# Layer 2's input weights decoded from layer 1's second tile pair on, and layer 1's third pair summed in one group

## The chip, the core and the metric

One core of a Trainium2 chip runs the whole program. The metric is the device time of one execution in microseconds (us); runs are compared by their median. TensorE (PE) multiplies, VectorE (DVE) and ScalarE (ACT) do the elementwise work, GpSimd (POOL) copies a little at the start, and nearly all transfers are issued by SyncE (SP) on one queue.

## The reference, cut to what matters

Three stages follow each other. Chunked attention (4 batches, 8 heads, 768 positions, chunks of 32 with a small context) gives x of 3072 tokens by 512. Two feed-forward layers of the same form follow, each with its own weights:

```
x = attention(q, k, v, mem_k, mem_v)            # 3072 x 512
h = x @ moe_w_in;   g = h * clip(h + 3, 0, 6) / 6;                x = g @ moe_w_out
h = x @ moe2_w_in;  g = where(h >= 1, h, where(h <= -1, 0, (h + 1)**2 / 4));  out = g @ moe2_w_out
```

w_in is 512 x 2048 and w_out 2048 x 512. The weights reach the kernel as float64 words, and TensorE is given pairs of fp32r tiles, a high part and the rest (hi, lo), so that each product is three matmuls: hi by hi, hi by lo, lo by hi.

## The kernel before, in words

**Tiles.** The tokens are 6 tiles of 512. Tiles 0 and 1 of layer 1 go through it plainly while attention for the later tiles runs between them. From tile 2 on, two tiles are taken as a pair, and each product with w_in is made with 7 instead of 8 block products (`PRODUCTS`: A11, S1, S2, A12, S3, S4, A22, where the S are sums of blocks). The pairs are named (layer, pair): (0, 1), (0, 2), (1, 0), (1, 1), (1, 2), with layer 1 as 0 and layer 2 as 1. "Layer 1's second tile pair" is (0, 1), its third (0, 2), and the first of layer 2 is (1, 0).

**f pairs.** The 2048 hidden columns are 16 blocks f of 128, taken two at a time: 8 f pairs, 0 to 7. `hidden_pair` makes one f pair: 7 products of 6 matmuls (L1027 to L1029) into PSUM banks `ph`, three copies by ACT (L1010), three additions by DVE (L1014), and four gates (`gate`: ACT L1074, in layer 2 also L1078, and DVE L1082). The banks of one product are taken again by a later one, so TensorE waits where a copy or an addition has not yet read a bank.

**The way out.** Pair (0, 1) multiplies each gated tile with w_out plainly (`project`, L902 to L904, after a split into hi and lo by ACT L886 and DVE L887). The other four pairs are in the table `SEVEN`: they keep their gated tiles g (up to 16 of them, in the pool of 32 slots `w` that also holds weights, raw words and operands) and sum w_out with 7 products too (`out_pair`, matmuls L1264 to L1266, block sums L1224, splits L886 and L887). `SEVEN` says in which groups of f pairs that is done. Within a group each product runs over the group's f pairs into two PSUM banks `po`, and then both banks are read out into the sums `csum`: the first time by a copy (L1234 on ACT or L1236 on DVE), later by an addition on DVE (L1242). Before the change (0, 2) has two groups of four f pairs: four f pairs, their way out, four f pairs, their way out.

**Decoding.** Layer 2's weights are decoded while layer 1 runs. `weight_pair(i)` takes f pair i of w_in: two loads of raw words (L318), a shift (L325 on ACT or L327 on DVE), a rescaling (ACT L331), a join (DVE L335), four differences (DVE L457), the casts (ACT L468, L471, L472) and the rests (DVE L469, L473, L476), and four stores to `wfs` (L482). `weight(1, f, 1)` does the like for w_out (casts on ACT at L303, rests on DVE at L366, stores L380), and `combine_out(i)` makes the block differences of w_out (DVE L496 and L510, ACT L509, stores L515). Nothing of this is multiplied before (1, 0) begins.

**What sets the order.** `Plan` is a list scheduler that runs when the program is built: every task has an engine or a choice of two, an estimated length, buffers, the tasks it depends on, and a key. Among what can start, the smaller key goes first. The result is one fixed order of instructions on each engine, and one queue of transfers on SP; at run time each engine takes its instructions in that order and waits where an input is late. A key counts in units of one plain f block; `base` is the key at which a pair begins, `NK` that of (0, 1), and `done[n, i]` is the last product of f pair i of the n-th pair.

Of the kernel before, what the change touches and what calls it, by code (L numbers as in the profile page):

```python
# [38 lines left out]
NK = 2 * NF  # L39
# [210 lines left out]
def dve(n, fast=False):  # L250
    return 70 + n / (1.92 if fast else 0.96)
# [10 lines left out]
def fused_kernel(ctx: ExitStack, tc: tile.TileContext, qkv, qk, vv, wpk, const, out):  # L262
# [31 lines left out]
    def tile_of(b):  # L294
        if b.tile is None:
            pool = ps if b.slot.pool in banks else smalls if b.slot.pool == "sm" else sb
            b.tile = pool.tile(b.shape, b.dtype, tag=f"{b.slot.pool}{b.slot.n}", name=b.name)
        return b.tile
# [3 lines left out]
    def cast(eng, out, in_):  # L302
        A.copy(out, in_) if eng == "ACT" else V.tensor_copy(out, in_)  # L303
# [6 lines left out]
    def words(raw):  # L310
        t = tile_of(raw)
        u = t.bitcast(U32).rearrange("p (n t) -> p n t", t=2)
        v = t.bitcast(F32).rearrange("p (n t) -> p t n", t=2)
        return u[:, :, 0], u[:, :, 1], v
# [34 lines left out]
    def weight(l, f, z, key, after=()):  # L349
        if l:  # L350
            raw = Buf(["w"], [128, 512], I64, "raw", ("raw", 4), w=1)
            w = Buf(["w"], [128, 2, 512], F32R, "w", ("wq", 4))
        else:
            raw = Buf(["w"] + ["lv"] * (f >= NF - 2), [128, 512], I64, "raw", w=6 if f < 6 else 1)
            w = Buf(["w"], [128, 2, 512], F32R, "w")
        w_buf[l, f, z] = w
        lo, hi = decoded(l, f, z, key, after, raw)

        to = (lambda h: by_chunk(tile_of(w)[:, h])) if l else (lambda h: tile_of(w)[:, h])
        of = (lambda: in_rows(words(raw)[2][:, 1])) if l else (lambda: words(raw)[2][:, 1])  # L360

        def high(e):
            cast(e, to(0), of())

        def low(e):
            V.tensor_tensor(out=to(1), in0=of(), in1=to(0), op=ALU.subtract)  # L366

        add(("ACT", 560), key - 0.2, high, [hi], [(w, 0)])
        t = add(("DVE", dve(512)), key - 0.1, low, [hi, (w, 0)], [(w, 1)])
        if l == 0:  # L370
            last_w.append(t)
        if l:
            keep(l, f, z, key + 1)
        return raw

    def keep(l, f, z, key, after=()):
        w = w_buf[l, f, z]
        to, of = (wos[l, f], ("wos", l, f)) if z else (wis[f], ("wis", f))
        add(
            ("SP", 430), key, lambda e: nc.sync.dma_start(to, tile_of(w).bitcast(F32)),  # L380
            [(w, 0), (w, 1)], [of], kb=512, after=after,
        )
# [681 lines left out]
    def gate(l, p, t, f, key, h, psum=False):  # L1064
# [22 lines left out]

    raw_g = {}
    SEVEN = {
        (0, 2): ((0, 1, 2, 3), (4, 5, 6, 7)), (1, 0): (tuple(range(8)),), (1, 1): (tuple(range(8)),), (1, 2): (tuple(range(6)), (6, 7)),  # L1090
    }
    BASE = (0, 29.25, 57.25, 85.25, 113.25)
    GMOST = 20
# [223 lines left out]
    for s in range(NS):  # L1317
        n, i = divmod(s, m)
# [36 lines left out]
    step = 2.75  # L1355
# [6 lines left out]
    done, w_of = {}, {}  # L1362
    pairs = [(0, 1), (0, 2), (1, 0), (1, 1), (1, 2)]
    for n, (l, p) in enumerate(pairs):
        base = NK + BASE[n]
# [37 lines left out]
            pair_x(*pairs[n + 1], base + 25, [done[n, 7 if seven else 5]], ["w"] if seven else ["in", "lv", "w"])  # L1403
        if n == 0:
            for i in range(NF // 2):
                weight_pair(i, base + 22 + 4 * i, [done[0, 5]])
        if n == 1:
            for i in range(NF // 2):
                raws = [weight(1, 2 * i + x, 1, base + 20 + step * (i + 0.5 * x) - 3, [done[1, 3]]) for x in range(2)]
                combine_out(i, raws, base + 20 + step * (i + 0.5) + 1)  # L1410

    with tc.manual_schedule():
# [98 lines left out]
```

## Time and profile before

| | |
|---|---|
| median of 3 runs | 1062.2 us (1061.84 to 1065.2) |
| the profiled execution's own time | 1067.35 us |
| its span, first to last instruction | 1065.3 us |
| granted TensorE clock, mean | 0.998 of full speed |

The profiled execution is a single one, taken with the profiler on. Its span is 2.05 us shorter than its own time, and its own time is 5.15 us above the median; times within the profile are counted from the span's start.

### The profile page before, as it was taken

The numbers are of one execution on the slowest core, as the hardware profiler recorded it, in microseconds if no ns is written. First come the engines' busy times: TensorE is split into PE (matmuls) and PEld (weight loads), VectorE is DVE, ScalarE is ACT, GpSimd is POOL, SyncE is SP. The second block draws the span as 40 slices with busy tenths as digits, with TensorE's granted clock in tenths as the row PEclk, the third lists the DMA queues.
The fourth block names the chain that finished last, engine by engine and source line by source line (L and its number), as shares of the span: only waits on it lengthen the run. The fifth ranks groups of instructions, "written<-read, shape, count | busy, mean of one in ns | idle before, by whom it ended". The sixth has DMA issues, their size and how long they took to land.

```text
span 1065.3 us, 19872 instructions
## 1 busy us (share of the span) xinstructions
PE 1036.6 (97%) x7381; PEld 842.6 (79%) x7381; DVE 835.9 (78%) x1439; ACT 679.8 (64%) x1427; POOL 27.2 (3%) x49
## 2 busy tenths in 40 slices
PE   6899999999999999999999999999999999999998
PEld 5677787788878887878778788888888888888886
DVE  4897489856876689789899997799765899658654
ACT  5897457634655586666785698655577655676461
POOL 4220000000000000000000000000000000000000
PEclk9999999999999999999999999999999999999999
DMA  8999878873988689999899799855774755965603
GB/s 244 345 358 359 332 237 273 285 243 112 321 282 258 198 300 368 417 399 390 309 404 399 282 344 391 311 178 188 228 266 151 282 169 177 334 223 198 191 34 79
DMA packets 153760, 289.18 MB, mean 271 GB/s; under 512 B 12352, under 2 KB 97984, under 8 KB 153664
## 3 DMA queue, kind: packets, MB, share of 16 engines
q1 hardware_dynamic: 153232, 287.62, 76.9%
q8 instruction: 58, 0.95, 0.4%
q10 hardware_dynamic: 432, 0.30, 0.1%
q14 instruction: 38, 0.31, 0.1%
HBM read 206.08 MB, written 81.79 MB: 270 GB/s over the span
## 4 chain that ended last, share of the span: by engine, by line
PE 67%; DVE 16%; DMA 11%; ACT 3%; issue 2%; SPq 1%; POOL 0%; DVEq 0%; POOLq 0%; ACTq 0%
PE ph L1027 10%; PE ph L1028 9%; PE ph L1029 9%; PE po L1265 7%; PE po L1266 7%; PE po L1264 7%; DMA raw<-wpk 5%; DVE glo L887 4%; PE py L902 3%; PE py L904 3%; PE py L903 3%; DVE raw L335 2%; PE ph L866 2%; DVE g L1224 2%; PE ph L868 2%
## 5 line engine op out<-in xcount | busy, mean ns | idle before, releaser
L886 ACT CAST ghi<-g 128x512 fp32r<-128x512 f32 x234 | 145.0, 621 | 119.1 <-PE po L1266 78.8
L887 DVE TENSOR_TENSOR glo<-g,ghi 128x512 fp32r<-128x512 f32 x234 | 158.7, 686 | 37.5 <-ACT ghi L886 37.2
L1027 PE MATMUL ph<-xop,wf 128*128 128x512 f32 x448 | 175.2, 391 | 3.2 <-DVE s L1014 1.9
L1028 PE MATMUL ph<-xop,wf 128*128 128x512 f32 x448 | 174.5, 390 | 0.8 <-DVE xop L977 0.8
L1029 PE MATMUL ph<-xop,wf 128*128 128x512 f32 x448 | 174.4, 389 | 0.0
L1265 PE MATMUL po<-glo,ws 128*128 128x512 f32 x420 | 163.6, 390 | 0.4 <-DVE glo L887 0.4
L1266 PE MATMUL po<-ghi,ws 128*128 128x512 f32 x420 | 163.4, 389 | 0.0
L1264 PE MATMUL po<-ghi,ws 128*128 128x512 f32 x420 | 163.4, 389 | 0.0
L1074 ACT ACTIVATE r<-s,bias 128x512 f32<-128x512 f32 x120 | 86.6, 724 | 58.7 <-DVE s L1014 57.8
L1014 DVE TENSOR_TENSOR s<-s,ph 128x512 f32<-128x512 f32 x120 | 81.8, 685 | 43.4 <-PE ph L1029 36.5
L1027 PEld LDWEIGHTS ph<-xop,wf 128*128 128x128 f32 x448 | 84.1, 188 | 24.1 <-DVE s L1014 4.2
L902 PE MATMUL py<-ghi,w 128*128 128x512 f32 x256 | 102.5, 401 | 0.0
L1010 ACT COPY s<-ph 128x512 f32<-128x512 f32 x120 | 70.6, 588 | 47.7 <-PE ph L1029 43.8
L903 PE MATMUL py<-glo,w 128*128 128x512 f32 x256 | 100.2, 391 | 0.2 <-DVE glo L887 0.2
L904 PE MATMUL py<-ghi,w 128*128 128x512 f32 x256 | 99.9, 390 | 0.0
L1028 PEld LDWEIGHTS ph<-xop,wf 128*128 128x128 f32 x448 | 84.1, 188 | 18.0 <-DVE xop L977 1.2
L1029 PEld LDWEIGHTS ph<-xop,wf 128*128 128x128 f32 x448 | 84.1, 188 | 17.6
L1265 PEld LDWEIGHTS po<-glo,ws 128*128 128x128 f32 x420 | 78.8, 188 | 17.6 <-DVE glo L887 1.2
L1264 PEld LDWEIGHTS po<-ghi,ws 128*128 128x128 f32 x420 | 78.8, 188 | 16.5
L1266 PEld LDWEIGHTS po<-ghi,ws 128*128 128x128 f32 x420 | 78.9, 188 | 16.1
L1082 DVE SCALAR_TENSOR_TENSOR g<-r,s 128x512 f32<-128x512 f32 x104 | 71.5, 690 | 24.3 <-ACT r L1078 10.1
L1224 DVE TENSOR_TENSOR g<-g 128x512 f32<-128x512 f32 x120 | 81.1, 687 | 1.4
(132 smaller groups left out, 1775.1 us busy)
## 6 DMA issues: line engine op xcount, KB each, us to landing
raw<-wpk SPq DMA_DIRECT2D x64, 512.0 KB
ws<-wcs SPq DMA_DIRECT2D x60, 512.0 KB
wf<-wfs SPq DMA_DIRECT2D x48, 512.0 KB
ws<-wos SPq DMA_DIRECT2D x90, 256.0 KB
wf<-wfs SPq DMA_DIRECT2D x48, 384.0 KB
wos<-w SPq DMA_DIRECT2D x32, 512.0 KB
wcs<-wc SPq DMA_DIRECT2D x32, 512.0 KB
w<-wos SPq DMA_DIRECT2D x32, 512.0 KB
```

Source lines behind the costliest of these rows:

```text
L886: add(("ACT", act(T)), key, lambda e: A.copy(tile_of(ghi), g()), [of], [(ghi, 0)], line="split")
L887: add(("DVE", dve(T)), key + 0.1, lambda e: V.tensor_tensor(out=tile_of(glo), in0=g(), in1=tile_of(ghi), op=ALU.subtract,), [of, (ghi, 0)] ...
L902: P.matmul(y, w2hi, gh, start=first, stop=False)
L903: P.matmul(y, w2hi, gl, start=False, stop=False)
L904: P.matmul(y, w2lo, gh, start=False, stop=last)
L1027: P.matmul(q, whi()[:, m], xh, start=first, stop=False, skip_group_check=True)
L1028: P.matmul(q, whi()[:, m], xl, start=False, stop=False, skip_group_check=True)
L1029: P.matmul(q, wlo()[:, m], xh, start=False, stop=c == 1, skip_group_check=True)
L1224: ("DVE", dve(T)), key, lambda e: V.tensor_tensor(out=o(), in0=i0(), in1=i1(), op=op),
L1264: P.matmul(q, wt[:, 0, m], xh, start=begin, stop=False, skip_group_check=True)
L1265: P.matmul(q, wt[:, 0, m], xl, start=False, stop=False, skip_group_check=True)
L1266: P.matmul(q, wt[:, 1, m], xh, start=False, stop=end, skip_group_check=True)
```

## The change

Three places change. `SEVEN` gives (0, 2) one group of all eight f pairs, so that its eight f pairs come first and its way out after them, as in (1, 0) and (1, 1). `weight_pair` gets smaller keys, wider apart, and may begin when f pair 0 of (0, 1) is done instead of f pair 5. The raw words of layer 2's w_out get smaller keys and may begin after f pair 1 of (0, 2) instead of f pair 3; `combine_out` keeps its keys.

```
     SEVEN = {
-        (0, 2): ((0, 1, 2, 3), (4, 5, 6, 7)), (1, 0): (tuple(range(8)),), ...
+        (0, 2): (tuple(range(8)),), (1, 0): (tuple(range(8)),), ...
...
         if n == 0:
             for i in range(NF // 2):
-                weight_pair(i, base + 22 + 4 * i, [done[0, 5]])
+                weight_pair(i, NK + 6 + 6 * i, [done[0, 0]])
         if n == 1:
             for i in range(NF // 2):
-                raws = [weight(1, 2 * i + x, 1, base + 20 + step * (i + 0.5 * x) - 3, [done[1, 3]]) for x in range(2)]
+                raws = [weight(1, 2 * i + x, 1, base + 14 + 3.2 * (i + 0.5 * x) - 3, [done[1, 1]]) for x in range(2)]
                 combine_out(i, raws, base + 20 + step * (i + 0.5) + 1)
```

TensorE has the same number of instructions before and after, in another order. Three places of the new order follow; rows that begin with - stand only in the order before, rows with + only in the new one.

The first is DVE in (0, 1), at its f pairs 1 and 2. L438 belongs to the weights of (0, 2), L420 to the next of these, L782 and `tr` to attention, and `raw` and `wp` are layer 2's w_in:

```order
+L335 SCALAR_TENSOR_TENSOR raw<-raw 128x512
+L887 TENSOR_TENSOR glo<-s,ghi 128x512
+L1014 TENSOR_TENSOR s<-s,ph 128x512
+L335 SCALAR_TENSOR_TENSOR raw<-raw 128x512
+L457 TENSOR_TENSOR raw<-raw 128x256 x2
+L1082 SCALAR_TENSOR_TENSOR g<-r,s 128x512
+L457 TENSOR_TENSOR raw<-raw 128x256 x2
+L335 SCALAR_TENSOR_TENSOR raw<-raw 128x512
+L303 COPY tr<-tp 128x512
+L1082 SCALAR_TENSOR_TENSOR g<-r,ph 128x512
+L469 TENSOR_TENSOR wp_3788<-raw,wp_3757 128x1024
 L1014 TENSOR_TENSOR s<-s,ph 128x512
```

Between two additions that TensorE's banks wait for there were no rows of layer 2 before; now there are joins, differences and a rest of 1024 columns.

The second is DVE on the way out of (0, 2). Before, in its second group:

```order
L1224 TENSOR_TENSOR g<-g 128x512
L1242 SCALAR_TENSOR_TENSOR csum<-po,csum 128x512
L887 TENSOR_TENSOR glo<-g,ghi 128x512
L1242 SCALAR_TENSOR_TENSOR csum<-po,csum 128x512
L1224 TENSOR_TENSOR g<-g 128x512
L887 TENSOR_TENSOR glo<-g,ghi 128x512
L1224 TENSOR_TENSOR g<-g 128x512
```

After, in the one group:

```order
L887 TENSOR_TENSOR glo<-g,ghi 128x512
L366 TENSOR_TENSOR w<-raw,w 128x512
L335 SCALAR_TENSOR_TENSOR raw<-raw 128x512
L887 TENSOR_TENSOR glo<-g,ghi 128x512
L1224 TENSOR_TENSOR g<-g 128x512
L887 TENSOR_TENSOR glo<-g,ghi 128x512
L1236 TENSOR_SCALAR csum<-po 128x512
L887 TENSOR_TENSOR glo<-g,ghi 128x512
```

The read-outs of `po` come half as often (28 before, 14 after, of which DVE has 23 and 10), and some of w_out's decoding now stands between the splits.

The third is SP's queue in (0, 1), around the first loads L410 of `w` from `wis` (for (0, 2)'s weights). `wos` holds layer 1's w_out, `wf` operands of (0, 2), `q_sb` attention's queries. Before:

```order
L410 DMA w<-wis 128x1024 x2
L566 DMA wf_3780<-wts 128x1024
L566 DMA wf_3786<-wts 128x1024
L566 DMA wf_3788<-wis 128x1024
L566 DMA wf_3796<-wis 128x2x256
L574 DMA w<-wos 128x1024
L632 DMA q_sb<-qk 128x4x128
```

After:

```order
L410 DMA w<-wis 128x1024 x2
L482 DMA wfs<-wp_3757 128x1024
L482 DMA wfs<-wp_3788 128x1024
L482 DMA wfs<-wp_3778 128x768
L574 DMA w<-wos 128x1024
L632 DMA q_sb<-qk 128x4x128
L637 DMA q_sb<-qk 128x384
```

The stores of layer 2's w_in (and, elsewhere in the queue, its raw words) now stand between the transfers of attention and of layer 1's weights; one early load of (0, 2)'s operands goes later.

## Rows read from the trace of the kernel before

**Rows 1.** The page, part 1: the span, and each engine's busy time.

```profile
span 1065.3 us, 19872 instructions
PE 1036.6 (97%) x7381; PEld 842.6 (79%) x7381; DVE 835.9 (78%) x1439; ACT 679.8 (64%) x1427; POOL 27.2 (3%) x49
```

**Rows 2.** Windows by stage: stretch, length, busy us (instructions) by engine, clock, DMA share, GB/s.

```profile
core 0: us, PE busy (x) PEld busy (x) DVE busy (x) ACT busy (x) POOL busy (x), PEclk, DMA share, GB/s
271.10:324.10 53.00, 53.00 (x599) 42.22 (x601) 39.80 (x79) 31.35 (x93) 0.00 (x0) 1.00 0.89 301
324.10:377.50 53.40, 53.40 (x595) 43.27 (x594) 33.56 (x63) 30.53 (x90) 0.00 (x0) 1.00 0.73 227
377.50:434.70 57.20, 56.96 (x367) 45.97 (x366) 53.46 (x87) 43.35 (x74) 0.00 (x0) 1.00 0.94 351
434.70:476.00 41.30, 40.17 (x175) 32.41 (x174) 33.34 (x58) 28.13 (x47) 0.00 (x0) 1.00 1.03 407
476.00:523.60 47.60, 47.60 (x211) 39.43 (x210) 44.63 (x77) 32.34 (x55) 0.00 (x0) 1.00 0.93 342
523.60:554.80 31.20, 29.27 (x127) 23.30 (x126) 27.86 (x49) 25.29 (x44) 0.00 (x0) 1.00 1.05 403
554.80:605.40 50.60, 49.56 (x217) 40.30 (x216) 50.50 (x74) 28.74 (x44) 0.00 (x0) 1.00 0.92 353
605.40:652.50 47.10, 46.77 (x204) 38.17 (x205) 44.05 (x82) 44.25 (x76) 0.00 (x0) 1.00 0.95 353
671.50:757.30 85.80, 85.80 (x380) 70.89 (x380) 77.40 (x123) 48.05 (x75) 0.00 (x0) 1.00 0.62 214
```

**Rows 3.** TensorE's waits from 390 to 650 us: waiter, releaser, us in total, times, longest.

```profile
PE ph L1027 <- DVE s L1014: 1.9, 4, 0.7
PE ph L1027 <- ACT s L1010: 1.3, 1, 1.3
PE ph L1028 <- DVE xop L977: 0.8, 1, 0.8
PE po L1265 <- DVE glo L887: 0.4, 1, 0.4
```

**Rows 4.** Timeline of PE in f pair 2 of (0, 2): start, us, instruction, idle before.

```profile
468.02 0.39 PE L1029 MATMUL ph<-xop,wf 128*128 128x512 f32 x1
468.82 0.50 PE L1027 MATMUL ph<-xop,wf 128*128 128x512 f32 x1 [0.41 <-DVE s L1014]
```

**Rows 5.** Timeline of DVE at the same place.

```profile
466.33 1.22 DVE L469 TENSOR_TENSOR wp<-raw,wp 128x1024 fp32r<-128x1024 f32 x1
467.47 0.69 DVE L1082 SCALAR_TENSOR_TENSOR g<-r,s 128x512 f32<-128x512 f32 x1
468.08 1.28 DVE L1014 TENSOR_TENSOR s<-s,ph 128x512 f32<-128x512 f32 x2
```

**Rows 6.** Timeline of ACT before the longest of these waits, f pair 5 of (0, 2).

```profile
527.01 0.67 ACT L325 ACTIVATE raw<-raw 128x512 uint32<-128x512 uint8 x1 [1.98 <-DMA raw<-wpk]
530.99 0.58 ACT L1010 COPY s<-ph 128x512 f32<-128x512 f32 x1
```

**Rows 7.** Groups of DVE, 271.1 to 324.1 us: busy, mean ns, idle before, its releasers.

```profile
L438 DVE TENSOR_TENSOR wt<-q,wt 128x1024 fp32r<-128x1024 f32 x4 | 4.8, 1208 | 0.3 <-ACT wt L437 0.3
L1082 DVE SCALAR_TENSOR_TENSOR g<-r,s 128x512 f32<-128x512 f32 x3 | 2.1, 693 | 3.6 <-ACT r L1074 3.6
L303 DVE COPY tr<-tp 128x512 f32<-128x512 f32 x3 | 2.1, 689 | 2.3 <-PE tp L789 2.3
```

**Rows 8.** Groups of DVE over the whole span, same columns: the operations that move.

```profile
L335 DVE SCALAR_TENSOR_TENSOR raw<-raw 128x512 uint32<-128x512 uint32 x64 | 44.4, 705 | 2.7 <-ACT raw L331 2.5
L1242 DVE SCALAR_TENSOR_TENSOR csum<-po,csum 128x512 f32<-128x512 f32 x20 | 13.3, 684 | 0.0
L457 DVE TENSOR_TENSOR raw<-raw 128x256 f32<-128x256 f32 x32 | 12.4, 422 | 0.5
L469 DVE TENSOR_TENSOR wp<-raw,wp 128x1024 fp32r<-128x1024 f32 x8 | 9.8, 1220 | 0.0
L473 DVE TENSOR_TENSOR wp<-raw,wp 128x512 fp32r<-128x512 f32 x8 | 5.5, 685 | 0.0
L476 DVE TENSOR_TENSOR wp<-raw,wp 128x256 fp32r<-128x256 f32 x8 | 3.3, 418 | 0.0
```

More of the change, by code (lines that the diff above doesn't have):

```diff
@@ L1089, in fused_kernel @@
     SEVEN = {
-        (0, 2): ((0, 1, 2, 3), (4, 5, 6, 7)), (1, 0): (tuple(range(8)),), (1, 1): (tuple(range(8)),), (1, 2): (tuple(range(6)), (6, 7)),
+        (0, 2): (tuple(range(8)),), (1, 0): (tuple(range(8)),), (1, 1): (tuple(range(8)),), (1, 2): (tuple(range(6)), (6, 7)),
     }
@@ L1405, in fused_kernel @@
             for i in range(NF // 2):
-                weight_pair(i, base + 22 + 4 * i, [done[0, 5]])
+                weight_pair(i, NK + 6 + 6 * i, [done[0, 0]])
         if n == 1:
             for i in range(NF // 2):
-                raws = [weight(1, 2 * i + x, 1, base + 20 + step * (i + 0.5 * x) - 3, [done[1, 3]]) for x in range(2)]
+                raws = [weight(1, 2 * i + x, 1, base + 14 + 3.2 * (i + 0.5 * x) - 3, [done[1, 1]]) for x in range(2)]
                 combine_out(i, raws, base + 20 + step * (i + 0.5) + 1)
```

## The prediction, made before the change was run

> **What bounds the kernel now.** I read the page first: TensorE is busy for 1036.6 us of a span of 1065.3 [rows 1], so a change that leaves its work alone can only shorten the gaps between its matmuls. Where they are, the windows by stage show; I set their bounds at DVE's additions L1014, so that a stage holds whole f pairs. Undisturbed, 380 matmuls take 85.80 us (way out of (1, 0)), 0.2258 us each [rows 2]. A stage without attention loses its length less its matmuls at that price: f pairs 0 to 2 of (0, 2), 41.3 - 175 x 0.2258 = 1.8 us; its first way out, 0.0; f pairs 4 to 6, 2.5; second way out, 1.6; f pairs 0 to 4 of (1, 0), 1.0 [rows 2]. That is 6.9 us in 218, and nearly all that such a change can win. The two stages of (0, 1) ahead of it show no idle TensorE at all (53.00 of 53.00, 53.40 of 53.40) [rows 2].
>
> The waits say who is late: DVE's additions, ACT's copies, DVE's operands for (1, 0), DVE's splits [rows 3]. Two places show how. In f pair 2 of (0, 2) a matmul starts 0.80 us after the one before it, 0.41 of it idle, waiting for an addition [rows 4]; that addition was ready earlier, but stood behind a rest of layer 2's w_in (L469, 1.22 us) and a gate [rows 5]. In f pair 5 ACT waited 1.98 us for late raw words, everything behind that slipped, and the copy L1010 came at 530.99 [rows 6]; this is the wait of 1.3 us in [rows 3]. So decoding that stands in front of an addition or a copy is what costs, and it costs where DVE is nearly full: 50.50 us busy of 50.60 in the second way out, 27.86 of 31.20 before it [rows 2]. DVE has room in (0, 1): 39.80 of 53.00 and 33.56 of 53.40 [rows 2].
>
> **What an instruction of DVE costs.** Two additions in a row take 1.28 us together [rows 5], while one alone is 0.685; the second starts 0.60 after the first, so in a full queue a row costs about 0.9 of its length. I use that factor on sums of rows that I count in the new order.
>
> [...]
>
> **The change, part by part.**
>
> *One group for (0, 2).* Seven products are read out once instead of twice: 28 read-outs become 14, on DVE 23 become 10. 13 x 0.684 [rows 8] x 0.9 = 8.0 us of DVE go. On the new way out, from the first addition of f pair 7 to the first of (1, 0), I count 90.4 us of rows, 81.4 in time, against 378 matmuls, 85.3 us: 95% full, with 11.8 us of rows of w_out's decoding in it. The way out of (1, 0) ran at 77.40 of 85.80 without loss, the old second group at 50.50 of 50.60 with 1.6 lost [rows 2]. I take 0.7, between 0 and 1.6. The matmuls are the same; a longer group costs TensorE nothing by itself. It holds 16 tiles g instead of 8, in 32 slots; (1, 0) does that already, without loss on its way out.
>
> *w_in earlier.* Each f pair of w_in is 2 joins, 4 differences and three rests on DVE: 2 x 0.705 + 4 x 0.422 + 1.220 + 0.685 + 0.418 [rows 8] = 5.4 us of rows. In the new order three f pairs stand in the stretch 271.1 to 324.1 (f pairs 1 to 3 of (0, 1)), where none was: 16.3 us of rows come, 2.1 leave (one L438 and two copies `tr` [rows 7] move out, small ones move in), net 14.2 x 0.9 = 12.8. DVE would have 39.8 + 12.8 = 52.6 us of work in 53.0. In the next stretch 5.1 of rows come, 33.56 + 4.6 = 38.2 of 53.4. The stretch of f pairs 0 to 2 of (0, 2) loses 12.0 of rows and is left with 33.34 - 10.8 = 22.5 us for 39.5 of matmuls, so its 1.8 us should go entirely.
>
> What hides the 12.8 us is DVE's idle time in (0, 1); if DVE lags there, the next thing late is an addition, so a bank, so TensorE. I counted it addition by addition: rows of DVE between two additions x 0.9, against TensorE's work between the products that they read. In the old order DVE's surplus never exceeds 2.0 us in (0, 1), and TensorE shows no idle there [rows 2]. In the new one it has 41.3 us against 37.3 from the first addition of f pair 1 to the second of f pair 3, and with 0.6 carried in reaches 4.5. What exceeds the 2.0 that cost nothing is my price: 2.5 us. The bounds are 0 and 12.8.
>
> The transfers: a pair of w_in is two loads of 512 KB and stores of 2 x 512 and 2 x 384 KB, 2.9 MB. Three pairs more in the 106 us of the two stretches are 81 GB/s on top of 301 and 227, so some 380 and 310; the stage from 434.7 sustained 407 [rows 2]. DMA is close to full but not over; I price nothing, and leave late raw words to the range.
>
> *w_out earlier.* Its decoding fills f pairs 2 to 6 of (0, 2), which now follow each other without a way out between them. f pairs 3 to 6 have 40.7 us of rows, 36.6 in time, for 168 matmuls, 37.9 us: 97% full. The nearest row is 523.6 to 554.8, the same mix, 27.86 of 31.20 with 2.5 lost in three f pairs [rows 2], 1.3 of it by the late raw words [rows 3, 6]. I take 1.5; bounds 0.5 and 3.3 (2.5 x 4/3). Less is left for (1, 0): its first five f pairs have 44.2 us of rows instead of 50.1, and I halve its 1.0 to 0.5.
>
> **The sum.** Before 1.8 + 0.0 + 2.5 + 1.6 + 1.0 = 6.9 us. After: 2.5 in (0, 1), 0 + 1.5 in (0, 2), 0.7 on its way out, 0.5 in (1, 0): 5.2. The difference is -1.7 us. The profiled execution took 1067.35 us in its own time (span 1065.3 [rows 1] and 2.05 around it), and would take 1065.6; it lies 5.15 above the median of the runs, and on that median, 1062.2, the forecast is 1060.5 us. The three runs of before lie 0.3% apart, so 0.3% (3.2 us) is about what this measurement can tell from no change; 1.7 is inside it.
>
> **Rivals.**
>
> *The backlog in (0, 1) is absorbed.* Between its products TensorE has plain projections and attention to do, and half of DVE's idle time there is waiting: 3.6 us of gates for ACT, 2.3 us of `tr` for TensorE [rows 7]; a DVE that runs late finds these inputs ready. Then (0, 1) loses 0, f pairs 3 to 6 lose 0.5, and after is 1.7: -5.2 us, 1057.0. For it: surpluses of up to 2.0 cost nothing before. Against: 99% full for 53 us, and a surplus of 1 to 1.6 us was enough for stalls in (0, 2).
>
> *DVE cannot use its idle time in (0, 1): slower.* Place: 271 to 324. The 13.2 us in which DVE is idle there are waits for inputs in a chain DVE, ACT, DVE, and ACT gets shifts, rescalings and casts of the same three f pairs on top of 31.35 us [rows 2]. If the waits stay, the decoding adds to the stretch instead of filling it. At 70% of 12.8, 9.0 us are lost: -6.9 + 2.7 + 9.0 = +4.8, 1067.0. It decides (slower by more than 3.2) from a loss there of 7.4, 58% of the added work. For it: that fullness, and late raw words that stop a whole engine [rows 6]. Against: the way out at 50.50 of 50.60 lost only 1.6 [rows 2].
>
> *Each operation of DVE costs its full row: slower.* Then f pairs 1 to 3 of (0, 1) have 57.3 us in 53.0, f pairs 3 to 6 of (0, 2) 40.7 in 37.9, the way out 90.4 in 85.3: 4.3 + 2.8 + 5.1 + 0.5 - 6.9 = +5.8, 1068.0. The two additions in 1.28 us [rows 5] speak against it. [...]
>
> **How the numbers follow.** Forecast 0.42, absorbed 0.36, idle time of no use 0.20, full rows 0.02. The likeliest case's own range is 1059.0 to 1063.0. The range of 1056.5 to 1067.0 reaches to the middle of both neighbours, which leaves out some 0.2: what is faster than the absorbed case, and the upper half of the slower ones. Faster by over 0.3% is 0.36, within it 0.42, slower 0.22.
>
> **What would show it.** In the profile after: TensorE idle at f pairs 1 to 4 of (0, 1), some 2.5 us in all, released by L1014, L1010 or an input of them; DVE over 95% busy there; no idle at f pairs 0 to 2 of (0, 2); few waits on the one way out, and 14 read-outs. The prediction is wrong on the fast side if (0, 1) still shows none, on the slow side if it shows over 7 us, or if TensorE waits for `ws`, `wf` or `w` that DMA brought late, which I have priced at nothing.

## The result, and the profile after

| | before | after |
|---|---|---|
| median | 1063.63 us of 6 runs (1060.82 to 1065.59) | 1074.97 us of 6 runs (1072.88 to 1076.54) |
| profiled execution, own time | 1067.35 us | 1073.35 us |
| its span | 1065.3 us | 1071.2 us |

The ratio is 1.0106, 95% interval 1.0085 to 1.0128: the change costs 11.3 us, where -1.7 was forecast and 1067.0 was the top of the range. The two profiled executions lie only 6.0 us apart, since that of before is a long one of its kind and that of after a short one; the ratio is what counts, and the profile says where.

The page of after, part 1, answers to [rows 1]. TensorE and its weight loads have as many instructions as before:

```profile
span 1071.2 us, 19868 instructions
PE 1041.9 (97%) x7381; PEld 845.4 (79%) x7381; DVE 829.1 (77%) x1427; ACT 680.0 (63%) x1425; POOL 27.9 (3%) x49
```

The windows by stage of after answer to [rows 2]. In this order: f pairs 1 to 3 of (0, 1); its f pairs 4 to 7; the change-over to (0, 2); f pairs 0 to 2 of (0, 2); 3 to 6; the way out; (1, 0)'s f pairs; its way out:

```profile
core 0: us, PE busy (x) PEld busy (x) DVE busy (x) ACT busy (x) POOL busy (x), PEclk, DMA share, GB/s
269.30:325.20 55.90, 54.10 (x613) 42.10 (x614) 50.52 (x103) 42.59 (x111) 0.00 (x0) 1.00 0.99 349
325.20:380.60 55.40, 54.22 (x589) 43.32 (x583) 38.16 (x75) 32.64 (x94) 0.00 (x0) 1.00 1.00 329
380.60:440.40 59.80, 58.25 (x367) 47.27 (x366) 50.99 (x80) 42.45 (x70) 0.00 (x0) 0.97 0.92 343
440.40:479.90 39.50, 39.50 (x176) 32.70 (x175) 23.37 (x39) 20.91 (x35) 0.00 (x0) 1.00 0.73 270
479.90:520.20 40.30, 39.24 (x171) 31.54 (x170) 35.66 (x65) 28.48 (x49) 0.00 (x0) 1.00 0.99 362
520.20:610.30 90.10, 88.24 (x380) 70.28 (x379) 81.69 (x127) 55.31 (x89) 0.00 (x0) 1.00 0.88 318
610.30:658.20 47.90, 47.55 (x210) 38.92 (x209) 39.93 (x69) 42.28 (x72) 0.00 (x0) 1.00 1.02 388
677.30:763.00 85.70, 85.70 (x379) 70.83 (x378) 77.35 (x122) 48.06 (x75) 0.00 (x0) 1.00 0.63 214
```

The first two stages, which took 53.0 and 53.4 us without a gap, take 55.9 and 55.4, and TensorE stands idle in both. DVE, at 50.52 of 55.90, is not full. The DMA engines are: 0.99 and 1.00, against 0.89 and 0.73. f pairs 0 to 2 of (0, 2) lose nothing any more (39.50 of 39.50), as forecast. The change-over ahead of them, for which the sum of the prediction has no term, takes 59.8 us in place of 57.2. f pairs 3 to 6 lose 40.3 - 171 x 0.2258 = 1.7, the way out 90.1 - 380 x 0.2258 = 4.3.

For the comparison of all kernels below, the trace gives the start of the first matmul L1027 of each f pair. Lengths between such starts, in us:

| kernel | (0, 1) | f pair 0 of (0, 2) | its f pairs 1, 2 | f pair 3 to f pair 1 of (1, 0) | ratio to before (95%) |
|---|---|---|---|---|---|
| before | 145.5 | 51.4 | 26.3 | 138.0 | |
| after | 150.3 | 54.1 | 24.5 | 139.6 | 1.0106 (1.0085 to 1.0128) |
| e1_group | 146.5 | 50.6 | 26.3 | 140.8 | 1.0047 (1.0028 to 1.0065) |
| e2_w_in | 154.4 | 54.6 | 24.5 | 138.2 | 1.0080 (1.0065 to 1.0096) |
| e3_w_out | 146.2 | 50.6 | 26.0 | 141.6 | 1.0054 (1.0032 to 1.0076) |
| e4_group_w_out | 146.7 | 50.6 | 26.8 | 143.1 | 1.0061 (1.0039 to 1.0083) |
| e7_group_w_in | 153.7 | 55.0 | 24.5 | 141.5 | 1.0115 (1.0084 to 1.0147) |
| e8_w_in_w_out | 154.7 | 53.5 | 24.5 | 137.3 | 1.0063 (1.0037 to 1.0090) |
| e5_short_dma | 145.8 | 50.3 | 24.5 | 139.8 | 1.0011 (0.9997 to 1.0025) |
| e9_short_loads | 146.9 | 50.3 | 24.5 | 140.2 | 1.0010 (0.9993 to 1.0026) |
| e10_short_stores | 145.9 | 50.3 | 24.5 | 139.3 | 0.9997 (0.9980 to 1.0013) |
| e6_short_dve | 156.5 | 62.7 | 24.5 | 139.5 | 1.0220 (1.0192 to 1.0247) |
| e11_short_dve2 | 153.3 | 51.5 | 24.5 | 139.7 | 1.0085 (1.0053 to 1.0116) |
| e13_q_pool | 155.3 | 51.8 | 24.5 | 138.0 | 1.0127 (1.0103 to 1.0151) |
| e17_extra | 165.7 | 51.6 | 26.8 | 138.0 | 1.0201 (1.0172 to 1.0229) |
| e12_w_in_mid | 145.7 | 57.5 | 24.7 | 137.1 | 1.0037 (1.0018 to 1.0056) |
| e15_all_spread | 157.3 | 52.5 | 24.5 | 141.3 | 1.0121 (1.0089 to 1.0152) |
| e16_w_in_spread | 157.4 | 54.4 | 24.5 | 138.0 | 1.0130 (1.0102 to 1.0159) |
| e14_short_out | 156.0 | 53.6 | 24.5 | 139.2 | 1.0108 (1.0072 to 1.0144) |
| e18_short_out_loads | 155.8 | 51.8 | 24.5 | 136.6 | 1.0063 (1.0041 to 1.0085) |

From f pair 1 of (1, 0) to the end all of them take 456.4 to 458.1 us. The (0, 1) of after, e14 and e18 has the same instructions, and took 150.3, 156.0 and 155.8 us: single executions of a stage that waits for transfers differ by 6 us, so that lengths of one execution are read together with the ratios. The last stretch varies less: the seven kernels with the same instructions in it (after, e5, e6, e9, e10, e11, e13) took 138.0 to 140.2 us.

**What is late in (0, 1).** The waits of after from 265 to 400 us, transfers only (waiter, releaser, us in total, times, longest):

```profile
ACT q_sb L303 <- DMA q_sb<-qk: 7.2, 3, 3.7
DVE q L420 <- DMA w<-wis: 4.9, 3, 2.5
ACT raw L325 <- DMA raw<-wpk: 2.4, 2, 1.9
DVE raw L327 <- DMA raw<-wpk: 2.0, 1, 2.0
ACT raw L331 <- DMA raw<-wpk: 1.8, 1, 1.8
```

With three smaller ones that is 21.0 us, against 10.2 in the kernel before (3.6 for `q_sb` and 2.9 for `w` the largest). `q_sb` is attention's, `w` belongs to the weights of (0, 2): transfers of attention and of layer 1 come late beside those of w_in's decoding. That the one makes the other late is what the experiments test. ACT and DVE take their instructions in order, so what stands behind such a wait is late too: gates, splits, copies. TensorE's own waits in the same stretch, which before had none there, name these:

```profile
PE ph L1027 <- DVE g L1082: 1.5, 2, 1.0
PE py L902 <- ACT ghi L886: 1.0, 1, 1.0
PE sc L748 <- DVE s L1014: 0.6, 1, 0.6
PE py L903 <- DVE glo L887: 0.6, 1, 0.6
PE ph L1027 <- ACT s L1010: 0.5, 1, 0.5
```

**How much the DMA engines can move here.** The summary of the transfers of the kernel before, in 265 to 385 us and then in the stage 434.7 to 476, from which the prediction took its 407 GB/s:

```profile
DMA packets 19544, 32.86 MB, mean 274 GB/s; under 512 B 1536, under 2 KB 13790, under 8 KB 19529
...
DMA packets 5580, 16.82 MB, mean 407 GB/s; under 512 B 588, under 2 KB 1100, under 8 KB 5578
```

In (0, 1) 71% of the packets are under 2 KB, in the other stage 20%. [rows 2] already had the consequence: 301 GB/s at a share of 0.89 is 338 at a full one, and 227 at 0.73 is 311; the prediction asked for some 380 and 310. After shows what was to be had, 349 and 329 at 0.99 and 1.00, so that what the division gives was some 5% low. The mix had changed too: 58% and 65% of the packets of these two stages of after are under 2 KB. The Trainium skill (DMA: Bandwidth & Descriptors, "Why small descriptors are slow (HBM only)") has a fixed cost on each packet, which weighs more on small ones; the trace agrees in the direction, 338 GB/s at a full share against 395 (407 at 1.03). No run changes the size of the packets alone, so that it is their size that lowers the rate is not shown.

### The profile page after: what moved, and what is told of

Same layout as the page of the kernel before. It is cut to its first block, busy times and chain, and to the rows that moved or that the text cites. A ratio compares the mean times of both kernels' runs of the same rounds, so it can differ in the third digit from the quotient of the medians.

```text
span 1071.2 us, 19868 instructions
## 1 busy us (share of the span) xinstructions
PE 1041.9 (97%) x7381; PEld 845.4 (79%) x7381; DVE 829.1 (77%) x1427; ACT 680.0 (63%) x1425; POOL 27.9 (3%) x49
## 4 chain that ended last, share of the span: by engine, by line
PE 44%; DVE 5%; DMA 3%; ACT 1%; SPq 0%; issue 0%; DVEq 0%; ACTq 0%
PE ph L1027 7%; PE ph L1028 7%; PE ph L1029 7%; PE po L1265 7%; PE po L1266 7%; PE po L1264 7%; DVE glo L887 2%; DMA raw<-wpk 2%; DVE g L1224 1%; DMA ws<-wcs 1%; DMA ws<-wos 1%; DVE xop L977 0%; PE po L1179 0%; PE po L1177 0%; PE po L1178 0%
## 5 line engine op out<-in xcount | busy, mean ns | idle before, releaser
L1027 PE MATMUL ph<-xop,wf 128*128 128x512 f32 x448 | 174.9, 390 | 1.4 <-DVE s L1014 0.8
L1265 PE MATMUL po<-glo,ws 128*128 128x512 f32 x420 | 164.4, 391 | 1.7 <-DVE glo L887 1.6
L1014 DVE TENSOR_TENSOR s<-s,ph 128x512 f32<-128x512 f32 x120 | 81.9, 683 | 49.6 <-PE ph L1029 48.0
L1027 PEld LDWEIGHTS ph<-xop,wf 128*128 128x128 f32 x448 | 84.1, 188 | 21.1 <-DVE s L1014 1.9
L1265 PEld LDWEIGHTS po<-glo,ws 128*128 128x128 f32 x420 | 78.8, 188 | 21.0 <-DVE glo L887 4.6
L1082 DVE SCALAR_TENSOR_TENSOR g<-r,s 128x512 f32<-128x512 f32 x104 | 71.5, 689 | 18.3 <-ACT r L1078 10.7
```

Source lines behind the costliest of these rows:

```text
L1027: P.matmul(q, whi()[:, m], xh, start=first, stop=False, skip_group_check=True)
L1265: P.matmul(q, wt[:, 0, m], xl, start=False, stop=False, skip_group_check=True)
```

## The experiments

The theories named in the expectations: A and later T, that w_in's decoding costs by its transfers in (0, 1); B, that the one long way out costs; V, that VectorE is overfull in (0, 1). The expectations speak of four pieces of w_in and of the 11 MB that their decoding moves: these are four of its eight f pairs, those due in (0, 1). The edits reach all eight, 23.1 MB (loads 8.4, stores 14.7); in the trace of after the loads of four and the stores of three are issued by 361 us, the rest from 380 to 438. The edits of the first two groups are against the kernel before, those of the others against the changed kernel unless something else is said.

### Each part alone, and two by two

e1 has the first of these edits, e2 the second, e3 the third; e4 the first and third, e7 the first and second, e8 the second and third:

```
-        (0, 2): ((0, 1, 2, 3), (4, 5, 6, 7)), (1, 0): ...
+        (0, 2): (tuple(range(8)),), (1, 0): ...
...
-                weight_pair(i, base + 22 + 4 * i, [done[0, 5]])
+                weight_pair(i, NK + 6 + 6 * i, [done[0, 0]])
...
-                raws = [weight(1, 2 * i + x, 1, base + 20 + step * (i + 0.5 * x) - 3, [done[1, 3]]) for x in range(2)]
+                raws = [weight(1, 2 * i + x, 1, base + 14 + 3.2 * (i + 0.5 * x) - 3, [done[1, 1]]) for x in range(2)]
```

> Only the grouping is changed: the third pair sums w_out over all eight f pairs in one group; both keys stay as before, so the decoding has the same due times as before. The first way out (before 38 us from 480 to 518) is gone and the second one holds 14 read-outs. Theory A (the loss of the whole change comes from w_in's decoding in the second pair, through transfers that come late there): this kernel stands within 3 us of before, since nothing moves in the second pair. Theory B (the loss comes from one long way out whose read-outs and residual sums queue on VectorE): this kernel is slower by 3 us or more, all of it between 480 and 610 us.

1069.24 us, ratio 1.0047: not within 3 us of before as A said, and (0, 1) within 1 us of before. The loss that the trace shows lies on the way out and at (1, 0)'s start (140.8 against 138.0), where B put it; these 2.8 us are not all of the 5.0 that the ratio stands for.

> Only w_in's key is changed: layer 2's w_in is decoded from the second f pair of the second pair on; the two groups and w_out's key stay. Theory A: the second pair takes 4 to 8 us longer than before, its share of the DMA engines stands at 0.95 or more, the f pairs 0 to 2 of the third pair lose nothing, and the whole is 3 to 8 us slower than before. Theory B: the second pair's loss is made up in the third, where VectorE has less to do, and the whole is within 3 us of before.

1072.78 us, ratio 1.0080: A's case, with 8.3 us just above its 3 to 8. f pairs 1 and 2 of (0, 2) gain 1.8 us, (0, 1) and f pair 0 lose several times that.

> Only w_out's key is changed (it is due earlier); w_in stays due late, so both matrices are decoded in the same stretch of the third pair. Theory A says nothing of a loss in the second pair here: it is as before within 1 us; in the third pair both decodings fall together and VectorE is the bound there, which costs 2 us or more. Theory B expects about the same time as before (within 2 us), since the two ways out stay.

1069.23 us, ratio 1.0054: (0, 1) as before, the third pair 3.6 us longer from its f pair 3 on (141.6), as A said of both decodings in one stretch. That VectorE is the bound there, as A also said, is not shown: from 526.5 to 600 us it is busy for 70.10 of 73.50 us, but the DMA engines are at 1.00.

> The group and w_out's key are changed, w_in's key is as before. Theory A: no loss in the second pair, so this kernel is faster than the whole change by 4 us or more. Theory B: as slow as the whole change or slower, because the one long way out stays and the third pair holds the decoding of both matrices.

1069.86 us, ratio 1.0061. Of the changed kernel's loss 0.0045 is gone, about 4.8 us, as A asked; what is left is in the last stretch, 143.1, the longest of all. Both theories hold a part.

> The one group and w_in's early decoding, with w_out's key as before. Theory T and V alike: the second pair loses as in the changed kernel (4 to 9 us). If w_out's key is what costs in the one way out, this kernel is 2 us or more faster than the changed one (ratio 1.0085 or less); if the grouping by itself costs, it stands at 1.010 to 1.013.

1074.52 us, ratio 1.0115: no faster than the changed kernel, so w_out's key is not what costs in it.

> Both early decodings with the two groups of before. If the one group costs what it did alone (4.7 us), this kernel is 3 us or more faster than the changed one (ratio 1.008 or less); if the one group costs nothing once w_in is out of the third pair, the ratio is 1.010 or more. Theories T and V both keep the loss of the second pair here.

1071.43 us, ratio 1.0063: with the two groups back the last stretch is 137.3 in place of 139.6, and the ratio 0.0043 lower, though the intervals touch. So w_in's move adds 0.0080 alone, 0.0068 beside the grouping, 0.0045 beside both others, but 0.0009 beside w_out's key alone; the grouping adds 0.0047 alone, 0.0035 and 0.0043 where w_in is moved, 0.0007 beside w_out's key alone. Each such difference of two ratios is uncertain by some 0.003.

### Transfers or VectorE

In e5 the packed words are loaded in 32 columns, and the shift and the rescaling behind them read a whole tile of constants in their place; stores are cut to 64 columns. e9 has the part on loads alone, e10 the part on stores (with the line on `wts`). All engines have the same instructions in the same order:

```
-            nc.sync.dma_start(tile_of(raw), wpk[l, f, z])
+            nc.sync.dma_start(tile_of(raw)[:, :cols], wpk[l, f, z][:, :cols])
...
-                    wfs[i, x, :, :m], flat(tile_of(b)).bitcast(F32)),
+                    wfs[i, x, :, :64], flat(tile_of(b)).bitcast(F32)[:, :64]),
...
-            src = [(wfs[i, x, :, :256 * shapes[x][0]], ("wfs", i, x)) for x in range(4)]
+            src = [(wts[i, x % 2, :, :256 * shapes[x][0]], ("wfs", i, x)) for x in range(4)]
```

> The changed kernel with the same instructions in the same order, but the transfers of w_in's decoding cut: the packed words are loaded in 32 of 512 columns, the finished pieces are stored in 64 columns, and layer 2 loads pieces of layer 1 in their place, so that the output is not the reference's. VectorE and ScalarE still work on whole tiles. Theory T (the second pair loses its time to transfers that come late because the DMA engines are full): the stretch from the second pair's first hidden matmul to the third pair's, 150.3 us in the changed kernel and 145.5 before, falls to 147 or less, its share of DMA to 0.8 or less, ScalarE's waits for q_sb and VectorE's for w shrink to those of before, and the whole comes to a ratio of 1.005 or less. Theory V (VectorE has too much work in the second pair, whenever the data comes): the stretch stays at 149 or more and the whole at 1.008 or more.

1064.72 us, ratio 1.0011: nearly the whole loss is gone, T's case: (0, 1) takes 145.8 us, and the waits for `q_sb` and `w` between 265 and 400 us are gone. (The DMA share, 0.81 and 0.85 between 269.3 and 380.6 us, stayed just above what was expected.)

> The changed kernel in the same order, with only the loads of w_in's packed words cut to 32 of 512 columns (4 of the 11 MB that the decoding moves; the stores of the finished pieces stay whole; the output is not the reference's). Theory T, in the form that any byte in the second pair costs the same: the ratio falls from 1.011 to about 1.007. In the form that the late piece is what VectorE and ScalarE themselves wait for (the packed words, raw): 1.004 or less. Theory V: 1.009 or more.

1065.43 us, ratio 1.0010: not the 1.007 of a price per byte, but the form of T in which the late piece is what counts.

> The changed kernel in the same order, with only the stores of w_in's finished pieces cut to 64 columns (7 of the 11 MB; loads whole; the output is not the reference's). By bytes alone the ratio falls to about 1.005; if what costs is that a piece's buffer isn't free until its store has landed, and that attention's q_sb stands behind the stores, to 1.003 or less; Theory V: 1.009 or more.

1065.13 us, ratio 0.9997, again below what bytes alone would give. Each part of the transfers alone gives all of the loss back, so it is not one of so much per byte: taking the loads away, 8.4 of the 23.1 MB, is enough. Windows from the first L1027 of f pair 1 of (0, 1) to that of its f pair 4, and from there to (0, 2), of the changed kernel and then of e10:

```profile
265.60:318.10 52.50, 50.70 (x520) 39.71 (x518) 48.16 (x98) 41.20 (x104) 0.00 (x0) 1.00 0.99 356
318.10:395.70 77.60, 76.42 (x868) 61.02 (x869) 57.00 (x109) 49.14 (x133) 0.00 (x0) 1.00 0.96 319
```

```profile
265.00:315.20 50.20, 50.20 (x519) 39.81 (x519) 47.96 (x98) 40.67 (x104) 0.00 (x0) 1.00 0.94 324
315.20:390.60 75.40, 75.40 (x869) 60.80 (x869) 58.74 (x113) 52.46 (x139) 0.00 (x0) 1.00 0.83 272
```

TensorE has no gap in e10, and DVE does the same work there in less time (47.96 of 50.20 us): it had room for it. The waits for transfers from 265 to 400 us, 21.0 us in the changed kernel, come to 1.5. One rival goes with this: SP's queue, too, takes its transfers in order, and in the changed kernel it stands up to 8.0 us before a store of w_in that waits for its cast (L468). In e10 it still stands up to 5.8 us there, with no loss, so that a stop of the queue is not by itself what costs.

In e6 and e11 the transfers are whole and DVE's work is cut. e11:

```
-                out=top, in0=top, scalar=3, in1=low, op0=ALU.logical_shift_left, op1=ALU.bitwise_or
+                out=top[:, :cols], in0=top[:, :cols], scalar=3, in1=low[:, :cols], op0=ALU.logical_shift_left, op1=ALU.bitwise_or
...
-            return lambda e: V.tensor_tensor(out=half(*out), in0=half(*a), in1=half(*b), op=ALU.subtract)
+            return lambda e: V.tensor_tensor(out=half(*out)[:, :32], in0=half(*a)[:, :32], in1=half(*b)[:, :32], op=ALU.subtract)
```

> The changed kernel in the same order with all of its transfers and each piece stored from its own buffer as in the changed kernel; VectorE's joins and the four differences between halves are cut to 32 columns (some 2.6 us less in each of four pieces of work; the output is not the reference's). Theory T: the second pair stays at 149 us or more and the ratio at 1.008 or more. Theory V: the second pair at 147 us or less, the ratio at 1.006 or less.

1072.74 us, ratio 1.0085, (0, 1) 153.3 us: T's case. In f pairs 1 to 3 DVE has 5.3 us less to do than in the changed kernel (42.83 against 48.16), and TensorE still waits:

```profile
264.10:317.10 53.00, 50.88 (x519) 39.83 (x517) 42.83 (x97) 40.82 (x104) 0.00 (x0) 1.00 1.00 353
```

e6, run before it, cut the shifts and the rests as well; since its rests are not whole, the stores of the low parts took the high parts' tiles:

```
-            out=two(bs[1]), in0=whole(), in1=two(bs[0]), op=ALU.subtract), [lo, hi, (bs[0], 0)], [(bs[1], 0)])
+            out=two(bs[1])[:, :, :16], in0=whole()[:, :, :16], in1=two(bs[0])[:, :, :16], op=ALU.subtract), [lo, hi, (bs[0], 0)], [(bs[1], 0)])
...
-                    wfs[i, x, :, :m], flat(tile_of(b)).bitcast(F32)),
+                    wfs[i, x, :, :m], flat(tile_of(bs[x & 2])).bitcast(F32)),
```

> The changed kernel with the same instructions in the same order and the same transfers, but VectorE's part of w_in's decoding cut to 32 of its columns (some 5 us less in each of four pieces of work; the output is not the reference's). Theory T: the stretch of the second pair stays at 149 us or more, since the transfers are all there. Theory V: it falls to 147 us or less and the whole to a ratio of 1.005 or less. If both this and the run with cut transfers give back half, both loads share the loss.

1087.19 us, ratio 1.0220. (0, 1) stays above 149 us, as T said, but this decides nothing: the edit added a wait of its own, seen in the waits from 290 to 450 us:

```profile
ACT wp L471 <- DMA wfs<-wp: 9.3, 1, 9.3
```

A tile is now read by two stores and free only after both, and a cast of ACT stood 9.3 us for it. The run says nothing on V, but shows what a late store does to an engine that takes its work in order.

### A queue, or the engines behind it

e13 (two lines like this one):

```
-                ("SP", 430), key - 6 - far, lambda e: nc.sync.dma_start(
+                ("SP", 430), key - 6 - far, lambda e: nc.gpsimd.dma_start(
```

> The changed kernel, but attention's queries and keys (q_sb) are loaded from GpSimd's queue in place of SP's, in the same program. If the transfers cost because q_sb is issued late, behind the decoding's transfers in SP's queue: ScalarE's waits for q_sb between 265 and 400 us (7.2 us in the changed kernel) fall to those of before (3.6) or less, and the ratio from 1.011 to 1.007 or less. If the DMA engines are simply full: other transfers are late in its place (w, raw, the buffers of wp) and the ratio stays at 1.009 or more.

1080.12 us, ratio 1.0127. The waits of e13 from 265 to 400 us:

```profile
DVE q L420 <- DMA w<-wis: 7.5, 2, 3.9
ACT wp L472 <- DMA wfs<-wp: 4.0, 1, 4.0
ACT raw L325 <- DMA raw<-wpk: 3.9, 1, 3.9
...
ACT q_sb L303 <- DMA q_sb<-qk: 1.8, 2, 1.2
```

`q_sb` comes in time, and what comes late in its place is `w`, `raw` and the stores. It is not `q_sb`'s place in the queue that costs; the DMA engines are full (0.98 from 269.3 to 380.6 us), and something else comes late. The Trainium skill (DMA: Bandwidth & Descriptors, "Issuing engines are not separate DMA queues") has the transfers of all issuing engines run on the same 16 DMA engines. This run agrees: with `q_sb` issued by another engine, `w` waited 7.5 us in place of 4.9.

e17, against the kernel before, with 10.5 MB that nobody reads:

```
-                    ("SP", 430), key - 4 + 0.1 * x, lambda e, x=x, w=w: nc.sync.dma_start(
-                        tile_of(w).bitcast(F32), wis[2 * i + x]),
+                    ("SP", 430), key - 4 + 0.1 * x, lambda e, x=x, w=w: (nc.sync.dma_start(
+                        tile_of(w).bitcast(F32), wis[2 * i + x]), nc.sync.dma_start(sink[4 + 2 * i + x], wpk[1, 2 * i + x, 0])),
```

and the same behind the stores of `wts`.

> The kernel before, with the same instructions on all engines in the same order, and 20 transfers more on SP's queue in the second pair: behind each of 8 loads of w_in's planes and 12 stores of combined pieces, 512 KB of packed words are copied from memory to memory, which nobody reads (10.5 MB, about as much as w_in's decoding moves). Theory T: the second pair takes 149 us or more (145.5 in the kernel before) and the ratio is 1.004 or more, though no engine has more to do. Theory V: within 0.2 per cent of before.

1086.69 us, ratio 1.0201: transfers alone are enough. They cost more than in the changed kernel, but these are copies from memory to memory, another kind than the loads and stores of the decoding, so that the two prices do not compare. Windows from the first L1027 of f pair 1 to that of f pair 4, and from there to (0, 2), and waits from 265 to 400 us:

```profile
267.00:332.10 65.10, 55.92 (x584) 43.70 (x583) 39.19 (x75) 29.95 (x86) 0.00 (x0) 0.90 0.90 323
332.10:412.60 80.50, 76.23 (x807) 60.11 (x806) 51.65 (x98) 48.09 (x133) 0.00 (x0) 1.00 0.88 301
```

```profile
ACT q_sb L303 <- DMA q_sb<-qk: 11.5, 3, 5.9
DVE q L420 <- DMA w<-wis: 11.3, 4, 5.9
...
PE ph L1027 <- ACT s L1010: 6.6, 1, 6.6
...
PE ph L1027 <- DVE g L1082: 2.9, 2, 2.6
```

DVE and ACT have the work of the kernel before in f pairs 1 to 3 (39.19 and 29.95 us; 39.16 and 30.05 there), are idle for 40% and 54% of the 65.1 us, wait for the same two tiles as in the changed kernel, and TensorE waits for them.

### Other places for w_in's decoding

e12 and e16 are against the kernel before, e15 (with e16's line) against the changed kernel:

```
-                weight_pair(i, base + 22 + 4 * i, [done[0, 5]])
+                weight_pair(i, NK + 18 + 5 * i, [done[0, 4]])
```

```
-                weight_pair(i, base + 22 + 4 * i, [done[0, 5]])
+                weight_pair(i, NK + 0 + 10 * i, [h_tasks[NK - 5]])
```

> The kernel before with w_in's decoding moved by less: its four pieces due 4, 3, 2 and 1 units earlier than before, from the fifth f pair of the second pair on, where the DMA engines of the kernel before were busy at 0.64 to 0.74 (340 to 380 us). Theory T: the second pair loses 2 us or less, the third gains up to 4 in its seven-product stretches, and the ratio is between 0.997 and 1.003. Theory V: the second pair takes over VectorE work where it has 30 per cent to spare, the same ratio; what it does in the third pair decides. A ratio above 1.005 would speak against both.

1067.95 us, ratio 1.0037, just above the expected range. (0, 1) loses nothing and the last stretch gains 0.9, but f pair 0 of (0, 2) takes 57.5 in place of 51.4: operands of (0, 2), `xraw` from `xmid`, come late. Little else moved: the rests L469 begin from 386 to 464 us, in the kernel before from 384 to 466, so that the run says little on a decoding in the second half of (0, 1). The waits of e12 from 390 to 404 us:

```profile
DVE xsum L963 <- DMA xraw<-xmid: 4.5, 1, 4.5
ACT xop L976 <- DMA xraw<-xmid: 4.1, 1, 4.1
PEld py L902 <- ACT ysb L932: 4.0, 1, 4.0
PE py L902 <- ACT ysb L932: 3.6, 1, 3.6
```

> The whole change, but w_in's four pieces are due from the end of the first pair on in steps of 10 units in place of 6 from its second f pair on; by SP's order one piece is decoded at the start of the second pair, where the DMA engines were busy at 0.29 to 0.76, and three from its last f pairs on. The theory that transfers in a full stretch cost and free stretches take them for nothing expects the second pair at 147 us or less and the ratio between 0.999 and 1.006, better than the whole change by 5 us; if only VectorE's backlog counted, 1.009 or more.

1079.76 us, ratio 1.0121: a miss, and the edit did not do what was expected of it. Not one f pair of w_in was decoded early but four: their loads were issued from 218 to 261 us, their rests L469 begin at 239, 250, 263 and 280, and the other four f pairs follow from 397 on. From 245 to 269.3 us the DMA share was 0.99 (0.41 before), and the first half of (0, 1) lost the time.

> The kernel before with w_in's four pieces due from the end of the first pair on in steps of 10 units; groups and w_out's key as before. Expected from the same theory: one piece in a stretch of free transfers costs nothing in the second pair (147 us or less), the third pair gains up to 2 us in its seven-product stretches, ratio 0.997 to 1.003. Above 1.005 would say that moving any of the decoding ahead costs by itself.

1080.74 us, ratio 1.0130: the same miss, with four f pairs decoded early again (rests from 241 to 282 us). It lies above the 1.005 that was to say that any move ahead costs by itself; with four at once the run can't say that, and one f pair alone in a free stretch was not tried. No version beats the kernel before.

### The one way out

e14 cuts DVE's work of w_out's decoding, e18 its loads (as in e9, for w_out). e14:

```
-                out=top, in0=top, scalar=3, in1=low, op0=ALU.logical_shift_left, op1=ALU.bitwise_or
+                out=top[:, :32 if l and z else 512], in0=top[:, :32 if l and z else 512], scalar=3, in1=low[:, :32 if l and z else 512], op0=ALU.logical_shift_left, op1=ALU.bitwise_or
...
-                    out=four(out()), in0=a(), in1=b(), op=ALU.subtract,
+                    out=four(out())[:, :, :, :8], in0=a()[:, :, :, :8], in1=b()[:, :, :, :8], op=ALU.subtract,
```

and e18:

```
-            nc.sync.dma_start(tile_of(raw), wpk[l, f, z])
+            nc.sync.dma_start(tile_of(raw)[:, :32 if l and z else 512], wpk[l, f, z][:, :32 if l and z else 512])
```

> The changed kernel in the same order, with VectorE's joins and differences between halves in the decoding of layer 2's w_out cut to a sixteenth (some 2.6 us less in each of four pieces of work, between 465 and 640 us; transfers whole; the output is not the reference's). If VectorE is what the one way out waits for: its loss (4.3 us between 520 and 610 us, plus 1.7 in the f pairs 3 to 6 before it) falls by 2 us or more, and the ratio from 1.011 to 1.0085 or less. If read-outs or transfers set it, the loss stays above 3.5 us and the ratio at 1.0095 or more.

1078.38 us, ratio 1.0108, and the last stretch 139.2 against 139.6: with less on DVE nothing is gained. By the same f pairs it has 5.7 us less in f pairs 3 to 6 (31.78 against 37.44) and 3.1 us less from f pair 7 on (85.87 against 88.93), which took 99.7 us against 99.6. DVE's load is not the cause there either.

> The changed kernel in the same order, with the loads of layer 2's packed w_out words cut to 32 of 512 columns (4 MB less between 465 and 615 us; VectorE and ScalarE work on whole tiles; the output is not the reference's). If transfers set the third pair's loss as they set the second's: the stretch from its f pair 3 to the fourth pair's f pair 1 falls from 139.6 us to 138 or less. If it is the order on ScalarE and VectorE (the fourth pair's operands between the splits of the read-outs): 139 or more, and the ratio stays at 1.009 or more.

1071.0 us, ratio 1.0063, 0.0043 below the changed kernel, though the intervals touch. The last stretch takes 136.6, below the 138.0 to 140.2 of the seven kernels with the same work there: transfers set some 3 us of it (139.6 - 136.6). From the first L1027 of f pair 7 to (1, 0)'s f pair 1, windows of the changed kernel and then of e18:

```profile
514.20:613.80 99.60, 97.74 (x421) 78.07 (x421) 88.93 (x140) 62.29 (x101) 0.00 (x0) 1.00 0.89 315
```

```profile
513.80:611.50 97.70, 96.35 (x421) 78.54 (x420) 88.64 (x139) 62.32 (x101) 0.00 (x0) 1.00 0.86 299
```

At 421 x 0.2258 = 95.1 the loss falls from 4.5 to 2.6 us. Of what is left, two stalls before L1265 of 1.1 and 0.7 us (start to start, less 0.2258) stay in their places in e18, with 1.1 and 0.6. ACT in the changed kernel shows the first:

```profile
583.06 0.62 ACT L886 CAST ghi<-g 128x512 fp32r<-128x512 f32 x1 [0.74 <-DVE glo L887]
585.60 1.05 ACT L976 CAST xop<-xraw 128x1024 fp32r<-128x1024 f32 x1 [1.91 <-DMA xraw<-ymid]
586.55 1.14 ACT L886 CAST ghi<-g 128x512 fp32r<-128x512 f32 x2
```

A cast of (1, 0)'s operands stands between two splits and waits 1.91 us for its input; the splits behind it, and DVE's behind those, are late by that, and TensorE waits at 588.56. That it is this wait that costs the 1.1 us is read from these rows; no run took it away.

## Why the prediction was wrong

**The step that failed** is the one that says of the transfers "DMA is close to full but not over; I price nothing". The addition (301 + 81 and 227 + 81, some 380 and 310) is sound; the ceiling was wrong. 407 GB/s was taken from a stage with 20% of small packets and set against one with 71%, where [rows 2] itself gives 338 and 311 at a full share, and after ran full at 349 and 329. e5, e9 and e10 take transfers away and the loss goes, e17 adds them and it comes, e11 takes DVE's work away and it stays. Its price is 0.0045 of the time (what e4 lacks) to 0.0109 (what e10 gives back), 4.8 to 11.6 us, where 0 stood. In the traces it is 4.4 us in (0, 1) and 3.8 in f pair 0 of (0, 2) (after less e10). The list of what would show it had the sign ("TensorE waits for `ws`, `wf` or `w` that DMA brought late"), but one level too near: not TensorE waited for transfers, but ACT and DVE did, and TensorE for them.

**DVE's backlog in (0, 1)**, forecast at 2.5 us, is nothing: in e10 DVE does all of it, busy for 47.96 of 50.20 us, and TensorE has no gap. That TensorE's idle time in the two stages of after comes to 3.0 us, close to the 2.5 looked for, is luck. Of the rivals, "absorbed" had DVE right; "full rows" falls with e10 too. "DVE cannot use its idle time" had the sign of the result, and even a price of the right size (9.0 us), by a mechanism that e10 and e11 rule out. What was looked for there, DVE over 95% busy and TensorE released by L1014, is not seen: DVE is at 90%, and of TensorE's waits L1014 ended 0.6 us and the gates L1082 1.5.

**f pairs 0 to 2 of (0, 2)** lose nothing, as forecast; f pairs 1 and 2 take 24.5 us in every kernel with w_in's early key. But the change-over ahead of them, at nothing in the sum without a word on it, took 2.6 us more (59.8 for 57.2); the two stalls of the last section fall there. **f pairs 3 to 6**: 1.7 us for 1.5.

**The one way out** was mis-sized: 4.3 us for 0.7, outside its bounds of 0 and 1.6. The working looked at DVE's fullness alone; e14 shows that this is not the limit. Late transfers are (e18: about 2 of the 4.5 us from f pair 7 on, 3 with the f pairs before it); (1, 0)'s operand casts between the splits are a likely other part, not shown by a run.

**The sum without the failed step.** With (0, 1) at nothing, f pairs 3 to 6 at 1.7, the way out at 4.3 and (1, 0) at 0.5, after loses 6.5 where before lost 6.9: next to no difference, and e10 measures 0.9997. So even with w_in's transfers for nothing the change would have gained little if anything: the forecast gain of 1.7 us (0.9984) lies at the edge of e10's interval (0.9980 to 1.0013), and outside those of e5 and e9.

What stays open: why the loss is not in proportion to the bytes, why w_in's early key and the grouping add so little beside w_out's key alone (0.0009 and 0.0007, each uncertain by some 0.003), and how much of the way out's remaining 2.6 us the operand casts hold.

## What to carry to other kernels

Before work is moved into a stage because an engine has room there, divide the stage's GB/s by its DMA share and see whether its own mix of transfers has room for the new ones (here that gave 338 and 311 where 349 and 329 came of it); a ceiling from a stage with another mix did not hold here. Late transfers need not show as waits of the engine that sets the end: here they stood one or two engines further back, where an instruction that waits for data holds up all that stands behind it. And cut one resource at a time with the order kept, and see in the trace that the edit did what it was meant to: two runs (e10 with transfers cut, e11 with elementwise work cut) settled what no reading of fullness could.

## What was not expected of the hardware

**Two stalls close together cost twice.** The windows of after around the first splits of (0, 2):

```profile
397.00:399.00 2.00, 0.90 (x3) 0.55 (x4) 2.00 (x3) 2.00 (x5) 0.00 (x0) 1.00 0.45 131
399.00:403.00 4.00, 4.00 (x12) 3.17 (x11) 3.93 (x9) 2.30 (x5) 0.00 (x0) 0.57 0.67 164
403.00:407.00 4.00, 4.00 (x19) 3.25 (x18) 2.56 (x4) 3.98 (x6) 0.00 (x0) 1.00 1.00 398
```

TensorE stood for two stalls of 1.1 and 0.9 us, and then the granted clock was 0.57 for 4 us: matmuls started 0.43 us apart (the lower of the two levels, 1.2 GHz) in place of 0.23. 12 matmuls ran where 19 run at the upper level, 7 x 0.2258 = 1.6 us on top of the 2.0 of the stalls. Together they are nearly all of what f pair 0 of (0, 2) takes more than in e10, 54.1 us against 50.3. Not every stall does this: after the one of 1.3 us in f pair 5 before the change [rows 3], and after the one of 1.1 us on the way out of after, the clock stayed at 1.00. In e17, with a stall of 6.6 us, the mean clock of f pairs 1 to 3 is 0.90.

**A loss that is not proportional.** Of w_in's 23.1 MB, taking away the 8.4 of the loads, the 14.7 of the stores or both gives the same time within the intervals (1.0010, 0.9997, 1.0011), where the changed kernel stands at 1.0106.
